# One 128-row weight transfer split into five transfers of 64, 24, 24, 8 and 8 rows, in a two-layer decode kernel on one core

## The chip, the core and the metric

The kernel runs on one core of one Trainium2 chip. The metric is device time in microseconds (us) of one launch; lower is better. The kernel before took 178.09 us, the median of three runs (177.34 to 178.23). The profile is of one more execution, whose own time was 177.7 us, with a span of 175.9 us from the first to the last instruction.

Five engines matter below: PE (matmul), DVE (vector), ACT (scalar), POOL, and SP, whose queue here does nothing but issue transfers from device memory (HBM) to on-chip memory (SBUF, 128 partitions). The transfers themselves are carried out by 16 DMA engines.

## What is computed

One token for each of four batch rows goes through attention and a gated feed-forward block, twice, with the same weights both times:

```python
def _A_ref(x, k_cache, v_cache, wq, wo):      # Hq 32, Hkv 8, Sk 8192, Dh 128; W = 2048
    q = (lambda x, *d: x.transpose(*d))((x @ wq).reshape(B, Sq, Hq, Dh), 0, 2, 1, 3)
    k = jnp.repeat(k_cache[:, :, Sk - W:, :], rep, axis=1)
    v = jnp.repeat(v_cache[:, :, Sk - W:, :], rep, axis=1)
    scores = jnp.einsum("bhqd,bhkd->bhqk", q, k) * (Dh ** -0.5)
    p = _softmax(scores, axis=-1)
    o = jnp.einsum("bhqk,bhkd->bhqd", p, v)
    return (lambda x, *d: x.transpose(*d))(o, 0, 2, 1, 3).reshape(B, Sq, Hq * Dh) @ wo
...
def _B_ref(x, w_gate, w_up, w_down):          # D 512, F 1792
    g = jnp.einsum("bsd,df->bsf", x, w_gate)
    u = jnp.einsum("bsd,df->bsf", x, w_up)
    h = _sigmoid(g) * u
    return jnp.einsum("bsf,fd->bsd", h, w_down)
...
x = x + _A_ref(_layernorm(x, axis=-1), A_k_cache, A_v_cache, A_wq, A_wo)
x = x + _B_ref(_layernorm(x, axis=-1), B_w_gate, B_w_up, B_w_down)
x = x + _A_ref(_layernorm(x, axis=-1), A_k_cache, A_v_cache, A_wq, A_wo)
x = x + _B_ref(_layernorm(x, axis=-1), B_w_gate, B_w_up, B_w_down)
```

Almost all the work is reading: 69.73 MB come from HBM in one launch. wq alone is 4 MB, each of the two cache windows 16 MB.

## The kernel before

The kernel is written as a list of operations with declared reads and writes (`P.op`, L52). A planner (`_schedule`, L92) puts them in an order for each engine, except for SP: there the transfers are issued in the order in which the code created them (L116 to L118). `_assign_sync` (L180) gives every SP transfer one of 24 semaphores in turn (L289) and lets a transfer wait until the one that used its semaphore before it, 24 transfers earlier, has landed (L197 to L202).

On-chip memory is an arena of 50 slots of 4 KB for each of 128 partitions. `tile_ap` (L384) is a pair of slots, 8 KB in each partition, 1 MB in all; `tok` (L387) names the two slots as what an operation writes or reads. Every transfer goes through `dma` (L396), which issues one `dma_start` at L399 on SP. So all SP transfers carry the line L399 in the profile.

A list `loads` holds the transfers that are still to be issued; `fill` (L450) issues from its head while there is a free tile. The list begins with the first read of wq (`load_wq(0)`, L1440), then comes K of the heads 0 to 2 (`load_k`, two 1 MB transfers each), then K, V and wo in turn (L1441 to L1450), the feed-forward weights, the second read of wq and so on. At the start the arena is empty, so that the first transfers are issued one behind the other with no wait.

The first read of wq is four blocks (`NC = 4`): block c holds rows 128c to 128c+127 of wq, one row of 4096 bfloat16 values (8 KB) in each partition. Each block is one transfer of 128 rows. `q_mms` (L793) multiplies: for block c, four matmuls of the normalised token (`xn`) with 512 columns each, at L804, accumulate over c. `q_first` (L826) runs this for the upper and lower half of the columns; the first four matmuls of a block wait for its transfer. Then come two transposes on DVE (L816), a multiply (L820), and on PE and ACT the spreading of q over the scores' layout (L851, L856). K tiles are transposed in place on DVE (L863), scores are built on PE (L881, L892), the softmax runs on DVE and ACT (L905 to L935), and P times V on PE at L982, which waits for V's transfers.

A tile that has been used up goes back to the pool and the next transfer of the list is issued into it, after a wait for the PE operation that read it last. From about 30 us on, most of SP's transfers wait in this way.

Of the kernel before, what the change touches and what calls it, by code (L numbers as in the profile page):

```python
# [254 lines left out]
class _SlotPool:  # L255
# [16 lines left out]
    bw_8k=421.0, bw_4k=409.0, bw_3k=405.0, bw_1k=347.0,  # L272
# [6 lines left out]
def build(nc, A_x, A_k, A_v, A_wq, A_wo, B_wg, B_wu, B_wd, out, cfg=None):  # L279
# [17 lines left out]
    NC = D // 128  # L297
# [15 lines left out]
    wq_d = A_wq.rearrange("(kt p) n -> p kt n", p=128)  # L313
# [9 lines left out]
    with es:  # L323
# [52 lines left out]
        def slot_ap(s):  # L376
            if s == SIDE:
                return side[:, 0:SLOT]
            return arena[:, s * SLOT:(s + 1) * SLOT]

        def stok(s, n=SLOT):
            return [("slot", s)] + (side_toks if s == SIDE else []) + ([("e", 0)] if s == SIDE and n > 1536 else [])

        def tile_ap(s):  # L384
            return arena[:, s * SLOT:(s + 2) * SLOT]

        def tok(s):  # L387
            return [("slot", s), ("slot", s + 1)]
# [7 lines left out]
        def dma(name, dst, src, w, r=(), rate="bw_4k", nbytes=None, sem=None):  # L396
            if nbytes is None:
                nbytes = dst.partition_size() * dst.free_nbytes()
            o = P.op("sync", name, 0.0, lambda e, dst=dst, src=src: e.dma_start(dst, src),  # L399
                     r=r, w=w, dma_bytes=nbytes, dma_rate=tm[rate])  # L400
            if sem is not None:
                o.sem = sem
                o.inc = 16
            return o


        loads = []
        where = {}
        left = {}
# [50 lines left out]
        def need(name):  # L460
            while name not in where:
                take_load()
            return where[name]

        def done(name):
            left[name] -= 1
            if left[name] == 0:
                s = where.pop(name)
                if name in on_free:
                    on_free[name](s)  # L470
                else:
                    pool.release(s)
                fill()
# [13 lines left out]
        def load_half(name, src, rate, size, where_):  # L487
            left[name] = 1
            homes[name] = [where_]
            on_free[name] = lambda s: hfree.add(s)  # L490

            def emit(s):
                dma(str(name), slot_ap(s)[:, 0:size], src, w=stok(s, size), rate=rate)
            loads.append((name, emit))

        def load(name, n_use, rate, part):
            left[name] = n_use

            def emit(s):
                src = part[1]  # L500
                dst = tile_ap(s)[:, 0:part[0]]
                if name[0] in ("wg", "wu"):
                    dst = tile_ap(s).rearrange("p (f n) -> p f n", f=2)[:, :, 0:F]
                elif len(src.shape) == 3 and not part[2]:
                    dst = dst.rearrange("p (f n) -> p f n", f=src.shape[1])
                dma(str(name), dst, src, w=tok(s), rate=rate)
            loads.append((name, emit))

        bounds = []
        f0 = 0  # L510
        while f0 < NFC:
# [9 lines left out]

        def load_wq(k):
            if k == 0:
                for c in range(NC):
                    load(("wq", c, k), 2, "bw_8k", (2 * SLOT, wq_d[:, c, :], False))
            else:
                for i in (1, 0):
                    for c in range(i, NC):
                        load_half(("wq", c, k, i), wq_d[:, c, i * SLOT:(i + 1) * SLOT], "bw_4k", SLOT,
                                  (((Y, 0), (Y, 1), (WQ, 1), (WQ, 0)), (None, (WQ, 0), (GA, 0), (SP, 0)))[i][c])  # L530

        def wq_part(k, c, i):

            if k == 0:
                return ("wq", c, k), i * SLOT
            return ("wq", c, k, i), 0
# [177 lines left out]
        o = P.op("scalar", "x_in", 1300.0, lambda e: e.dma_start(x_nat, x_d), w=[("prow",)])  # L714
# [78 lines left out]
        def q_mms(k, i, qb, cs):  # L793
            for c in cs:
                name, o = wq_part(k, c, i)
                s = need(name)

                src = slot_ap(s) if k else tile_ap(s)
                rd = stok(s) if k else tok(s)

                def e_q(pe, c=c, src=src, o=o):
                    last = None
                    for hh in range(4):
                        last = pe.matmul(ps[32 * hh:32 * hh + NB, qb, :], xn[:, c * NB:(c + 1) * NB],  # L804
                                         src[:, o + hh * 512:o + (hh + 1) * 512],
                                         start=(c == 0), stop=(c == NC - 1))
                    return last
                P.op("tensor", "q%d_%d_%d" % (k, i, c), 4 * tm["pe_row"], e_q,
                     r=rd + [("xn",)], w=[("qrow", i)], banks=(qb,))
                done(name)  # L810
# [15 lines left out]
        def q_first(variance):  # L826
            for n, i in enumerate((0, 1)):
                q_mms(0, i, OBS[n], range(NC))
                if n == 0:
                    variance()  # L830
                q_turn(0, i, OBS[n])

        def q_second(variance):
            q_mms(1, 1, WB, (0, 1))
            variance()
            unstash_half(tuple(named("ln_rd2Q")))
            q_mms(1, 1, WB, (2, 3))
            q_mms(1, 0, OBS[1], (0,))
            fresh.append(q_turn(1, 1, WB))
# [598 lines left out]
        stashed = ("V",) + keep[0] + (0,)  # L1438
        stay = keep[1:] + [(HKV - 2, 1)]
        load_wq(0)  # L1440
        for h in range(AHEAD):  # L1441
            loads.append((("K", h), lambda _, h=h: load_k(h)))
# [7 lines left out]
        load_wo(HKV // 2 - 1)  # L1450
        load_glu(0)
        load_wq(1)
        v_tiles = {}
        n_v = 0
# [16 lines left out]
        n = len(P.ops)  # L1471
# [44 lines left out]
def bass_interleave_layers__sliding_block_cached__glu_gated_glu__decode_kernel(  # L1516
    nc, A_x, A_k_cache, A_v_cache, A_wq, A_wo, B_x, B_w_gate, B_w_up, B_w_down, out,
):
    build(nc, A_x, A_k_cache, A_v_cache, A_wq, A_wo, B_w_gate, B_w_up, B_w_down, out)
# [28 lines left out]
```

## Time and profile before

| | us |
|---|---|
| median of three runs | 178.09 (177.34 to 178.23) |
| the profiled execution | 177.7 |
| its span | 175.9 |
| PE busy | 106.1 |
| DVE busy | 104.2 |
| ACT busy | 32.7 |
| POOL busy | 21.7 |
| bytes moved | 70.00 MB, mean 398 GB/s |

Busy time is time in which an engine executed instructions; waiting is not counted, nor is issuing a transfer. In the profile "L863 DVE" is an instruction of line 863 on DVE, and "arena<-in_A_wq_dram" is a transfer from wq into the arena. Beside this page the trace keeps one record for each packet that a DMA engine moved, with its queue, size, start and length, and the time of every semaphore update; a row of 8 KB is one packet, and each engine ends its part of a transfer with a packet of 4 bytes, the end mark that updates the semaphore. The lines on which the forecast rests are shown in it.

### The profile page before, as it was taken

What the parts mean: (1) busy time and instruction counts of PE and PEld (TensorE: products, weight loads), DVE (VectorE), ACT (ScalarE), POOL (GpSimd) and SP (SyncE); (2) the same over time, 40 slices, a digit from 0 to 9 for tenths busy, and PEclk for the clock granted to TensorE, in tenths of its full rate; (3) what the DMA queues carried; (4) which work ended last, traced back from release to release, by engine and by line L of the source; (5) the groups of instructions that cost most, each with busy time, mean ns of one, the idle gap of its engine ahead of it and who ended that gap; (6) DMA issues with size and microseconds to landing.
All of it is one profiled execution on the core that took longest, in us unless ns stands there. A gap on an engine that the chain in (4) does not pass through costs nothing.

```text
span 175.9 us, 3909 instructions
## 1 busy us (share of the span) xinstructions
PE 106.1 (60%) x1653; PEld 54.2 (31%) x1653; DVE 104.2 (59%) x256; ACT 32.7 (19%) x87; POOL 21.7 (12%) x89
## 2 busy tenths in 40 slices
PE   0536256269566282661765466547987999776663
PEld 0203112014334051340444452142322444425321
DVE  6307997994957748377322381316299999733351
ACT  2002022322303003020030000100133455430011
POOL 6100010101101001010010000000011553342000
PEclk9999999999999999999999999999999999965576
DMA  5999999999999999999999999999999999999990
GB/s 180 419 436 423 419 421 427 404 428 423 415 415 412 417 428 421 427 404 427 417 414 425 408 399 403 412 407 388 402 366 408 425 419 419 421 417 401 411 376 31
DMA packets 12738, 70.00 MB, mean 398 GB/s; under 512 B 1320, under 2 KB 1328, under 8 KB 6576
## 3 DMA queue, kind: packets, MB, share of 16 engines
q1 hardware_dynamic: 12712, 69.74, 97.4%
q8 instruction: 13, 0.21, 0.5%
q14 instruction: 5, 0.04, 0.1%
q10 hardware_dynamic: 8, 0.00, 0.0%
HBM read 69.73 MB, written 0.00 MB: 396 GB/s over the span
## 4 chain that ended last, share of the span: by engine, by line
DMA 47%; DVE 33%; PE 15%; issue 2%; SPq 1%; POOL 1%; ACT 0%; DVEq 0%
DMA arena<-in_A_v_cache_dram 19%; DMA arena<-in_B_w_down_dram 13%; DVE arena L863 12%; DMA arena<-in_A_wq_dram 10%; PE ps L892 7%; DMA arena<-in_B_w_gate_dram 5%; DVE small L905 5%; PE ps L881 2%; DVE arena L1073 2%; DVE small L909 2%; DVE side L913 2%; DVE side L940 2%; DVE arena L1078 1%; DVE arena L593 1%; DVE small L917 1%
## 5 line engine op out<-in xcount | busy, mean ns | idle before, releaser
L863 DVE STREAM_TRANSPOSE arena<-arena 128x1024 f32<-128x1024 f32 x32 | 37.0, 1205 | 0.1
L982 PE MATMUL ps<-side,arena 128*128 128x8 bf16 x576 | 18.2, 168 | 13.4 <-DMA arena<-in_A_v_cache_dram 13.4
L892 PE MATMUL ps<-arena,side 128*32 128x512 bf16 x256 | 25.2, 527 | 0.0
L982 PEld LDWEIGHTS ps<-side,arena 128*128 128x128 bf16 x576 | 16.8, 104 | 19.7 <-DMA arena<-in_A_v_cache_dram 17.2
L905 DVE TENSOR_REDUCE small<-ps 128x1 f32<-128x512 f32 x16 | 10.8, 676 | 17.6 <-PE ps L892 17.5
L920 ACT ACTIVATE side<-ps,small 128x512 bf16<-128x512 f32 x16 | 11.0, 687 | 36.7 <-PE ps L1000 18.4
L881 PE MATMUL ps<-small,msk_s 128*32 128x512 bf16 x64 | 8.6, 526 | 14.3 <-DVE arena L863 13.7
L856 ACT CAST side<-ps 128x256 bf16<-128x256 f32 x16 | 5.9, 370 | 34.7 <-PE ps L892 25.8
L892 PEld LDWEIGHTS ps<-arena,side 128*32 128x32 bf16 x256 | 8.3, 120 | 10.2 <-issue 7.5
L935 ACT CAST side<-ps 128x512 bf16<-128x512 f32 x16 | 9.4, 585 | 10.8 <-PE ps L933 10.8
L933 PE MATMUL ps<-side,perm 128*128 128x512 bf16 x16 | 8.1, 507 | 5.0 <-ACT side L920 4.9
L949 POOL CAST small<-small 128x1 bf16<-128x1 f32 x9 | 1.7, 187 | 76.2 <-ACT side L920 76.2
L804 PE MATMUL ps<-arena,xn 128*4 128x512 bf16 x60 | 7.7, 574 | 3.9 <-DMA arena<-in_A_wq_dram 3.6
L782 ACT ACTIVATE small<-ps 128x4 f32<-128x4 f32 x4 | 0.7, 173 | 47.8 <-PE ps L778 47.8
L1354 PE MATMUL ps<-arena,xn 128*4 128x448 bf16 x60 | 7.1, 530 | 3.1 <-DMA arena<-in_B_w_up_dram 1.5
L1064 PE MATMUL ps<-arena,side 128*32 128x512 bf16 x112 | 8.2, 416 | 0.2 <-DVE small L917 0.2
L940 DVE STREAM_TRANSPOSE side<-side 128x256 f32<-128x256 f32 x16 | 6.9, 433 | 2.2 <-ACT side L935 2.0
L851 PE MATMUL ps<-side,eyew 32*128 32x64 bf16 x64 | 5.6, 217 | 3.4 <-ACT side L856 2.4
L881 PEld LDWEIGHTS ps<-small,msk_s 128*32 128x32 bf16 x64 | 1.7, 98 | 17.2 <-DVE arena L863 15.8
L816 DVE STREAM_TRANSPOSE side<-ps 128x512 f32<-128x512 f32 x3 | 2.2, 717 | 8.2 <-PE ps L804 8.1
L990 DVE TENSOR_TENSOR onb<-ps,rinv 128x16 bf16<-128x16 f32 x9 | 1.7, 185 | 8.9 <-PE ps L982 8.6
L1363 DVE STREAM_TRANSPOSE side<-ps 128x448 f32<-128x448 f32 x4 | 2.5, 636 | 6.7 <-PE ps L1354 6.7
(119 smaller groups left out, 135.5 us busy)
## 6 DMA issues: line engine op xcount, KB each, us to landing
arena<-in_A_v_cache_dram SPq DMA_DIRECT2D x27, 1024.0 KB, 18.9
arena<-in_A_k_cache_dram SPq DMA_DIRECT2D x16, 1024.0 KB, 24.9
arena<-in_A_wq_dram SPq DMA_DIRECT2D x4, 1024.0 KB, 8.1
arena<-in_A_wo_dram SPq DMA_DIRECT2D x3, 1024.0 KB, 26.5
arena<-in_A_wq_dram SPq DMA_DIRECT2D x6, 512.0 KB, 6.3
arena<-in_B_w_up_dram SPq DMA_DIRECT2D x4, 448.0 KB, 6.2
arena<-in_B_w_gate_dram SPq DMA_DIRECT2D x2, 896.0 KB, 21.9
arena<-in_B_w_up_dram SPq DMA_DIRECT2D x2, 896.0 KB, 22.8
```

Of the source, the lines that this page charges most:

```text
L804: last = pe.matmul(ps[32 * hh:32 * hh + NB, qb, :], xn[:, c * NB:(c + 1) * NB], src[:, o + hh * 512:o + (hh + 1) * 512], start=(c == 0), s ...
L863: P.op("vector", "T%d_%d" % (h, t), c_dve(1024), lambda v, v32=v32: v.transpose(v32, v32), r=[("slot", 4 * h + t)], w=[("slot", 4 * h + t)])
L881: last = pe.matmul(ps[32 * gi:32 * gi + 32, bank, :], msk_s[:, :], msk_m[:, :].unsqueeze(1).broadcast_to([128, 256, 2]), start=True, stop= ...
L892: last = pe.matmul(ps[32 * gi:32 * gi + 32, bank, :], qbd[:, q0:q0 + 32], kt[:, cp // 2, cp % 2, jh * NJ:(jh + 1) * NJ, :], start=False, s ...
L905: lambda v: v.tensor_reduce(nmax[:, k2:k2 + 1], ps[:, bank, :], AXX, ALU.max),
L920: lambda a: a.activation(prow[:, :].rearrange("p (m x t) -> p m x t", x=32, t=2), ps[:, bank, :].rearrange("p (m t x) -> p m x t", x=32, t ...
L933: lambda pe: pe.matmul(ps[:, pb, :], perm[:, :], prow[:, :], start=True, stop=True),
L935: P.op("scalar", "pc" + tag, c_act(512), lambda a: a.copy(prow[:, :], ps[:, pb, :]), r=[("ppb", pb)], w=[("prow",)], banks=(pb,))
L940: P.op("vector", "pt" + tag, c_dve(256), lambda v: v.transpose(et, prow[:, :].bitcast(F32)), r=[("prow",)], w=[("e", k2)])
L982: last = pe.matmul(ps[:, ob, bp * 8:bp * 8 + 8], src[:, j * 128:(j + 1) * 128], ev[:, j % 2, j % 16 // 2, x0:x0 + 8], start=(j == 0), stop ...
L1064: last = pe.matmul(ps[32 * g:32 * g + 32, ob, :], ew[:, g, mq, t], src.rearrange("p (m t d) -> p t m d", t=2, d=128)[:, t], start=(n == 0) ...
L1354: last = pe.matmul(ps[32 * g:32 * g + NB, gub[n], 0:NF], xn[:, c * NB:(c + 1) * NB], slot_ap(s)[:, g * NF:(g + 1) * NF], start=(c == 0), s ...
```

## The change

The fourth block of the first read of wq (c = 3) no longer comes as one transfer of 128 rows. It comes as five, of the rows 0 to 63, 64 to 87, 88 to 111, 112 to 119 and 120 to 127, issued one behind the other in the place of the one, into the same tile and the same partitions as before. The first of them takes the place of the old one among the tokens (it "writes" both slots of the tile); the other four get tokens of their own, and the same dependencies as the first. The operation of PE that multiplies this block reads all five tokens, so it waits for five semaphores instead of one.

```diff
+        ROWS = (0, 64, 88, 112, 120, 128)
+
+        def load_rows(name, n_use, src):
+            left[name] = n_use
+
+            def emit(s):
+                first = None
+                for n, (a, b) in enumerate(zip(ROWS[:-1], ROWS[1:])):
+                    o = dma("%s_%d" % (name, a), tile_ap(s)[a:b, :], src[a:b, :], w=[("rows", n)] if n else tok(s), rate="bw_8k")
+                    if n:
+                        o.deps.update(first.deps)
+                    else:
+                        first = o
+            loads.append((name, emit))
...
             if k == 0:
-                for c in range(NC):
+                for c in range(NC - 1):
                     load(("wq", c, k), 2, "bw_8k", (2 * SLOT, wq_d[:, c, :], False))
+                load_rows(("wq", NC - 1, k), 2, wq_d[:, NC - 1, :])
             else:
...
                 rd = stok(s) if k else tok(s)
+                if not k and c == NC - 1:
+                    rd = rd + [("rows", n) for n in range(1, len(ROWS) - 1)]
```

On PE, DVE, ACT and POOL the same instructions stand in the same order in both kernels. On SP there are four transfers more, ahead of the first transfer of K; all that follow keep their order. As semaphores are dealt out in turn, every later transfer uses the one four places further on.

## The prediction

> **What bounds the kernel now.** I read the page from the top: busy shares, slices, transfer queues; then the table by stretches, the chain of waits in order of time, the first 20 us of the timeline, and the packet records.
>
> ```profile
> PE 106.1 (60%) x1653; PEld 54.2 (31%) x1653; DVE 104.2 (59%) x256; ACT 32.7 (19%) x87; POOL 21.7 (12%) x89
> DMA  5999999999999999999999999999999999999990
> GB/s 180 419 436 423 419 421 427 404 428 423 415 415 412 417 428 421 427 404 427 417 414 425 408 399 403 412 407 388 402 366 408 425 419 419 421 417 401 411 376 31
> q1 hardware_dynamic: 12712, 69.74, 97.4%
> q8 instruction: 13, 0.21, 0.5%
> q10 hardware_dynamic: 8, 0.00, 0.0%
> ```
>
> No engine is busy for more than 60% of the span; the 16 DMA engines are busy in every slice but the first and last, and SP's own queue (q1) alone fills 97.4% of them. The table by stretches (its columns: length, busy time of each engine, clock, DMA share, GB/s) shows where they are short of work:
>
> ```profile
> 13.30:63.00 49.70, 27.56 (x349) 12.23 (x350) 38.85 (x65) 9.80 (x24) 3.77 (x20) 1.00 1.01 420
> 90.00:120.00 30.00, 16.53 (x339) 11.22 (x340) 10.12 (x31) 1.31 (x5) 0.36 (x2) 1.00 1.02 409
> 120.00:135.00 15.00, 12.38 (x130) 4.12 (x130) 10.33 (x28) 3.91 (x11) 1.15 (x5) 1.00 1.01 387
> ```
>
> Only from 120 to 135 us does the rate fall clearly, to 387 GB/s against 420: (1 - 387/420) x 15 = 1.2 us of lost reading. Everywhere else a microsecond of DMA time lost is a microsecond of the kernel. The chain says how far ahead the queue runs (start, length, what):
>
> ```profile
> 2.19 11.09 DMA arena<-in_A_wq_dram
> 13.33 0.60 PE ps L804 x4
> 16.30 4.54 DVE arena L863 x4
> 63.98 22.92 DMA arena<-in_A_v_cache_dram
> 87.99 11.30 DMA arena<-in_A_v_cache_dram
> 116.47 6.65 DMA arena<-in_A_wq_dram
> 155.70 16.72 DMA arena<-in_B_w_down_dram
> ```
>
> The chain runs over DVE and PE from 13 to 64 us, but the transfer issued at 63.98 lands 22.92 us later: about nine transfers stand ahead of it, so a delay of DVE of a few us would cost nothing there. The depth shrinks to 6.65 us at 116 and is 16.72 us again at the end. What the end waits for, all the way, is the reading. The changed transfer is the fourth that SP issues. The timeline shows the issues and PE's waits for the blocks of wq (in brackets the idle time before, and what ended it):
>
> ```profile
> 0.79 2.03 SPq L399 DMA_DIRECT2D arena<-in_A_wq_dram  x4
> 2.86 6.21 SPq L399 DMA_DIRECT2D arena<-in_A_k_cache_dram  x8
> 8.36 0.10 PEld L804 LDWEIGHTS ps<-arena,xn 128*4 128x4 bf16 x8 [1.01 <-DMA arena<-in_A_wq_dram]
> 10.84 0.10 PEld L804 LDWEIGHTS ps<-arena,xn 128*4 128x4 bf16 x8 [2.37 <-DMA arena<-in_A_wq_dram]
> 13.33 0.09 PEld L804 LDWEIGHTS ps<-arena,xn 128*4 128x4 bf16 x4 [2.39 <-DMA arena<-in_A_wq_dram]
> ```
>
> Blocks land 2.48 us apart (10.84 - 8.36; 13.33 - 10.84 = 2.49): 128 rows on 16 engines are 8 rows each, 2.48 / 8 = 0.31 us a row, which is also the length of a row's packet (0.309). An engine has one row under way and begins the next 3 ns before the last ends. So the rows can be followed engine by engine, and **each engine is its own queue**: what delays one is made up nowhere unless it runs out of work. The 13 instruction reads of q8 show it: each holds one engine for about 1.05 us, the next row then takes 0.8 instead of 0.31, and that engine stays some 1.6 us behind. The 16 engines end the fourth block of wq within 0.4 us, but the last transfer between 170.98 and 173.06 us: eight within 0.6 us of the first, eight 1.4 to 2.1 us behind it. The semaphore waits for the last.
>
> **The change part by part.** The sum is made against the profiled 177.7 us (span 175.9 and 1.8 around it), which is 0.4 us under the median of 178.09.
>
> *Bytes:* the same 128 rows of 8 KB. *SP:* four issues more of 0.41 to 0.63 us (shortest and longest issue of wq), so K's first issue moves from 2.86 to 4.5 to 5.4 us; all transfers behind it move too, until the queue is full (the issue at 7.52 us already takes 1.5 us for that). The engines reach K at about 12.4 us: hidden by three blocks of wq. Without that cover it would be 1.6 to 2.5 us. *Semaphores:* each transfer now waits for one 24 places back in a list longer by four; the first such wait, at about 31 us, is for a block of wq landed at 6 us: nothing. *End marks:* four more of 9 ns on an engine: 0.04 us. *PE:* five semaphores instead of one ahead of the matmuls of c = 3; with 0.04 to 0.05 us an issue step (the chain's "issue" pieces), 0.2 us. Behind it stand L778 and the second half of L804, for which DVE's L816 waits: on the DVE chain, not on the reading.
>
> *Which engine moves what.* A 128-row transfer leaves 16 end marks with 8 rows to each. The x load (4 rows) leaves 8 packets in q10, four rows and four marks: one row on each of four engines. So a transfer is cut into equal shares. If 64, 24 and 8 rows are cut likewise (16 shares of 4, 12 of 2, 8 of 1) and always begin with the same engine, eight engines get 4+2+2+1+1 = 10 rows, four get 8 and four get 4: +0.62, 0 and -1.24 us. The trace shows no transfer of 24 or 8 rows. [...]
>
> *What a narrow transfer costs.* The disputed term. All large transfers here span 128 partitions. **Lower bound:** rows keep 0.31 us wherever they go, and only the shares above count: between -0.6 and +0.6 at the end (rivals). **Upper bound:** what limits a row is the way into its group of partitions, ways in proportion to rows; then every transfer, however narrow, takes the 2.48 us of a full one: 5 x 2.48 - 2.48 = +9.9. The nearest row is the x load: its four rows of 1 KB took 0.044 us, two at a time, about half of a 2-KB row (0.084), which speaks for the lower end; but 4 KB in all may rest in buffers that 512 KB does not fit. Between ends this far apart I take the middle, **+5.0 us**.
>
> [...]
>
> *Where it goes.* Eight engines have to take all five in turn and are then 5 us behind; each K, V and weight transfer lands when its last engine does. They never run dry before 120 us, so nothing is made up. The DVE chain starts with q and K, both later by the same 5 us. The 1.2 us lost from 120 to 135 belong to engines that had run ahead; the late ones do not gain there. Sum: 177.7 + 5.0 + 0.0 = 182.7, against the median 178.09 + 5.0 = **183.1; I say 183.0**, with 181.0 to 184.8 for this case.
>
> **The rivals.**
>
> *Rows only move between engines (no price for narrowness).* The end moves by the shares: if one of the late engines is among the eight, +0.62, if none, down. For it: the x packets. The two x engines that can be told by their starts (first wq row at 1.86 and 1.88 us, 6 ns behind an end mark of x) were, as far as packets can be followed, delayed by instruction reads, one at 88.2, the other at 125.4 and 144.2; and x's four engines belong to the eight if the cut begins with the same engine. So +0.2: 178.3 (177.7 to 178.9).
>
> *A smaller price.* Narrowness counts for the 64 rows alone (2.48 instead of 1.24: +1.24), the short ones overlap with K, plus the 0.62 of shares: 180.0 (179.0 to 181.0).
>
> *Faster.* Place: the end of each transfer. The late eight are the four engines relieved by 1.24 us and the four that are unchanged, the early eight those that get 0.62. Then the latest end moves from 2.1 to 1.5 us behind the first: -0.6; with a smaller spread part of the 1.2 us lost from 120 to 135 returns, -0.4 by a third of it: 177.1 (176.3 at most). It decides from the point where no late engine is among the eight. Against it: the two x engines above, and that instruction reads hit eight different engines one after the other before 120 us.
>
> **How the numbers follow.** A measurement of this kernel can tell about 0.5% (0.9 us) from no change. Chances: forecast 0.55, smaller price 0.12, rows only 0.22, faster 0.11. Slower by over 0.5% is the first two, 0.67; within 0.5% 0.22; faster 0.11. The range leaves out the faster case and some 0.07 above (the upper bound is 188, for which I see little): 177.6 to 184.8.
>
> **What would show it.** Right: the wait at L804 for the last block ends near 18 instead of 13.3 us; the GB/s of the first three slices falls; the landings of K all stand some 5 us later; eight engines' end marks lie 5 us behind the others for the rest of the run. Wrong: the wait ends at 13 to 14 us and row packets keep 0.31 us: then narrowness has no price, and the end marks' spread at 20 us (1.9 us in that case, 0.62 + 1.24) tells which engines are which.

## The result and the profile after

| | before | after |
|---|---|---|
| median of four runs each, us | 178.16 (177.34 to 178.49) | 184.03 (183.78 to 184.58) |
| ratio, 95% interval | | 1.0341 (1.0298 to 1.0383) |
| the profiled execution, us | 177.7 | 183.9 |
| its span, us | 175.9 | 182.2 |

The kernel is 5.9 us slower; the interval makes that 5.3 to 6.8 us. In the code after the change, L804 is now L822, L816 is L834, L863 is L881, L892 is L910 and L982 is L1000. From the page of the profile after, busy times, slices and SP's queue:

```profile
PE 106.7 (59%) x1653; PEld 54.6 (30%) x1653; DVE 104.2 (57%) x256; ACT 32.7 (18%) x87; POOL 21.7 (12%) x89
DMA  5999999999999999999999999999999999999990
GB/s 192 426 266 138 397 421 421 423 412 419 423 424 413 419 416 419 424 415 415 421 417 423 419 396 402 398 394 405 380 312 410 419 426 419 417 416 408 407 366 26
q1 hardware_dynamic: 12752, 69.74, 97.0%
```

The engines' work is what it was. SP's queue moved the same bytes, but its packets took 97.0% of 182.2 us = 176.7 us of 16 engines' time, against 97.4% of 175.9 = 171.3 before: 5.4 us more. The rate falls in the third and fourth slice (9.1 to 18.2 us), to 266 and 138 GB/s; the row "DMA" above it shows 9 all the same. Only one later slice stands out, the 30th (132 to 137 us), with 312 where before has 366. The table by stretches says it for the stretch in which the five transfers move. First the kernel before, then the one after (length, PE, PEld, DVE, ACT, POOL, clock, DMA share, GB/s):

```profile
11.00:19.20 8.20, 3.65 (x30) 1.38 (x22) 4.85 (x7) 1.12 (x4) 0.00 (x0) 1.00 1.01 426
```

```profile
11.00:19.20 8.20, 1.02 (x9) 0.14 (x9) 0.00 (x0) 0.00 (x0) 0.00 (x0) 1.00 1.00 181
19.20:30.00 10.80, 5.49 (x46) 2.20 (x46) 9.57 (x12) 1.49 (x5) 0.00 (x0) 1.00 1.01 421
120.00:135.00 15.00, 11.52 (x132) 4.96 (x132) 6.27 (x19) 1.90 (x6) 0.00 (x0) 1.00 1.03 382
```

A DMA share of 1.00 at 181 GB/s: the DMA engines always have a packet under way, but the packets take longer. Lost in these 8.2 us: (1 - 181/426) x 8.2 = 4.7 us. After it the rate is back, and from 120 to 135 us it is no better than the 387 of before: nothing is made up. The work of that stretch comes some 5.4 us later now, and from 125.4 to 140.4 us the rate is 368. The timeline of the kernel after shows SP's issues and PE's waits for the blocks of wq:

```profile
0.79 4.34 SPq L399 DMA_DIRECT2D arena<-in_A_wq_dram  x8
5.17 5.19 SPq L399 DMA_DIRECT2D arena<-in_A_k_cache_dram  x8
8.19 0.10 PEld L822 LDWEIGHTS ps<-arena,xn 128*4 128x4 bf16 x8 [0.84 <-DMA arena<-in_A_wq_dram]
11.11 0.10 PEld L822 LDWEIGHTS ps<-arena,xn 128*4 128x4 bf16 x8 [2.82 <-DMA arena<-in_A_wq_dram]
19.20 0.59 PE L822 MATMUL ps<-arena,xn 128*4 128x512 bf16 x4 [7.06 <-DMA arena<-in_A_wq_dram]
```

The third block is multiplied at 11.11 (before 10.84), the fourth at 19.20 (before 13.33): it comes 5.9 us later. The chain of waits carries that to the end, with the same links as before:

```profile
4.81 14.26 DMA arena<-in_A_wq_dram
22.17 4.54 DVE arena L881 x4
69.83 22.63 DMA arena<-in_A_v_cache_dram
93.55 11.31 DMA arena<-in_A_v_cache_dram
121.90 6.86 DMA arena<-in_A_wq_dram
163.23 15.53 DMA arena<-in_B_w_down_dram
```

Against before the links stand 5.9 us later at the first L881, the same at 69.83, 5.6 at 93.55, 5.4 at 121.90, and the last one lands at 178.76 against 172.42: 6.3. From the records of packets and semaphore updates, the length of a row's packet (8 KB; median) by when it began, and when the last engine's end mark came:

```
row packets that began in     10.5-12.5   12.5-15   15-17.5   from 20 us on
before                          309 ns     309 ns    309 ns        312 ns
after                           618 ns     819 ns   1104 ns        312 ns     (longest 1199 ns)

landing, us       block c=2   64 rows   24 rows   24 rows   8 rows   8 rows   first K
before              10.79     13.28 (128 rows)                                15.77
after               11.07     13.62     15.29     16.96     18.27    19.06    21.23
```

The 64 rows alone take as long as the whole block took. The other four add 1.68, 1.66, 1.32 and 0.79 us, which is 5.45 us; the first K transfer is 5.46 us late.

### The profile page after: what moved, and what is told of

It is laid out like the page before. It is cut to its first block, busy times and chain, and to the rows that moved or that the text cites. A ratio compares the mean times of both kernels' runs of the same rounds, so it can differ in the third digit from the quotient of the medians.

```text
span 182.2 us, 3918 instructions
## 1 busy us (share of the span) xinstructions
PE 106.7 (59%) x1653; PEld 54.6 (30%) x1653; DVE 104.2 (57%) x256; ACT 32.7 (18%) x87; POOL 21.7 (12%) x89
## 4 chain that ended last, share of the span: by engine, by line
DMA 47%; DVE 31%; PE 15%; issue 2%; SPq 2%; POOL 1%; ACT 0%; DVEq 0%
DMA arena<-in_A_v_cache_dram 19%; DMA arena<-in_B_w_down_dram 12%; DVE arena L881 12%; DMA arena<-in_A_wq_dram 12%; PE ps L910 7%; DVE small L923 5%; DMA arena<-in_B_w_gate_dram 5%; PE ps L899 2%; SPq L399 2%; DVE arena L1091 2%; DVE small L927 2%; DVE side L931 2%; DVE side L958 2%; DVE arena L1096 1%; DVE arena L609 1%
## 5 line engine op out<-in xcount | busy, mean ns | idle before, releaser
L881 DVE STREAM_TRANSPOSE arena<-arena 128x1024 f32<-128x1024 f32 x32 | 36.9, 1203 | 0.1
L1000 PE MATMUL ps<-side,arena 128*128 128x8 bf16 x576 | 18.2, 168 | 13.5 <-DMA arena<-in_A_v_cache_dram 13.5
L910 PE MATMUL ps<-arena,side 128*32 128x512 bf16 x256 | 25.8, 538 | 0.0
L1000 PEld LDWEIGHTS ps<-side,arena 128*128 128x128 bf16 x576 | 16.7, 104 | 19.9 <-DMA arena<-in_A_v_cache_dram 17.4
L822 PE MATMUL ps<-arena,xn 128*4 128x512 bf16 x60 | 7.6, 573 | 10.1 <-DMA arena<-in_A_wq_dram 9.8
L910 PEld LDWEIGHTS ps<-arena,side 128*32 128x32 bf16 x256 | 8.3, 121 | 10.3 <-issue 7.8
L953 ACT CAST side<-ps 128x512 bf16<-128x512 f32 x16 | 9.4, 585 | 10.5 <-PE ps L951 10.5
L834 DVE STREAM_TRANSPOSE side<-ps 128x512 f32<-128x512 f32 x3 | 2.1, 717 | 14.1 <-PE ps L822 14.0
```

The lines of the kernel that those rows point to most:

```text
L881: P.op("vector", "T%d_%d" % (h, t), c_dve(1024), lambda v, v32=v32: v.transpose(v32, v32), r=[("slot", 4 * h + t)], w=[("slot", 4 * h + t)])
L910: last = pe.matmul(ps[32 * gi:32 * gi + 32, bank, :], qbd[:, q0:q0 + 32], kt[:, cp // 2, cp % 2, jh * NJ:(jh + 1) * NJ, :], start=False, s ...
L953: P.op("scalar", "pc" + tag, c_act(512), lambda a: a.copy(prow[:, :], ps[:, pb, :]), r=[("ppb", pb)], w=[("prow",)], banks=(pb,))
L1000: last = pe.matmul(ps[:, ob, bp * 8:bp * 8 + 8], src[:, j * 128:(j + 1) * 128], ev[:, j % 2, j % 16 // 2, x0:x0 + 8], start=(j == 0), stop ...
```

## The experiments

All are the changed kernel with another cut of the fourth block of wq. `PARTS` below lists (rows, columns) of the transfers in the order of issue, with a:b written for a slice; SP issues them and PE waits for them as in the changed kernel, and all the rest is the same. The edit common to them, and then one list each:

```diff
-        ROWS = (0, 64, 88, 112, 120, 128)
+        PARTS = [...]
...
-                for n, (a, b) in enumerate(zip(ROWS[:-1], ROWS[1:])):
-                    o = dma("%s_%d" % (name, a), tile_ap(s)[a:b, :], src[a:b, :], w=[("rows", n)] if n else tok(s), rate="bw_8k")
+                for n, p in enumerate(PARTS):
+                    o = dma("%s_%d" % (name, n), tile_ap(s)[p], src[p], w=[("rows", n)] if n else tok(s), rate="bw_8k")
...
-                    rd = rd + [("rows", n) for n in range(1, len(ROWS) - 1)]
+                    rd = rd + [("rows", n) for n in range(1, len(PARTS))]
```

Three theories stood after the result. *Ways*, of the kind of the prediction's upper bound: rows that go at the same time to the same part of the 128 partitions share one way in, and each is slower by the number that share it (two on one way: twice 309 ns); how the partitions would be divided among ways no run shows. *Number*: each transfer costs something as such (about 1.5 us, 5.9 over four). *Shares*: what counts is that some engines get more rows than others. cols5, two64, eight16 and eight16s ran beside a kernel before with a median of 177.71 us, the other four beside one with 177.77.

**cols5: five transfers, each over all 128 partitions**

```diff
+PARTS = [(:, 0:2048), (:, 2048:2816), (:, 2816:3584), (:, 3584:3840), (:, 3840:4096)]
```

> The fourth block comes as five transfers again, but cut by columns: each spans all 128 partitions, with 4096, 1536, 1536, 512 and 512 bytes of every row. [...] Number: every transfer more costs the same, whatever its shape, (184.03 - 178.16) / 4 = 1.5 us: +5.9, 184.0. Shares: the cost came from engines with unequal numbers of rows; here all engines move the same: +0, 178.2.

178.66 us, ratio 1.0051 (1.0031 to 1.0070): +0.95 us. As many issues and semaphores as in the changed kernel, more end marks (80 against 56), and less than a sixth of its loss. In the table of slices of cols5 the dip is nearly gone:

```profile
GB/s 183 426 318 432 424 421 419 409 425 423 421 415 412 420 426 423 417 411 420 424 419 421 408 400 405 403 406 373 393 410 419 417 424 423 415 415 405 407 376 27
```

Number falls. By estimate from the packets of before (4 KB 0.159 us, 2 KB 0.084) the smaller pieces come to 8 x (0.159 + 2 x 0.065 + 2 x 0.03) = 2.8 us instead of 2.48, +0.3; the 0.95 is more than that. The packets say where it is: the pieces of 1.5 KB took 65 ns and those of 0.5 KB 27, but the 4-KB pieces of the first of the five took 245 ns in the mean, where other 4-KB packets take 159 at the median and 165 in the mean: 8 x 0.08 = 0.6 us or a little more for each engine. Why they do was not tried.

**two64 and four32: two or four transfers of neighbouring rows**

```diff
+PARTS = [(0:64, :), (64:128, :)]                                      # two64
+PARTS = [(0:32, :), (32:64, :), (64:96, :), (96:128, :)]          # four32
```

> The fourth block comes as two transfers, rows 0 to 63 and 64 to 127; every engine moves 4 rows of each. Ways: each of the two reaches half of the ways, so 8 rows pass each way in turn, 2.48 us a transfer: 4.96 instead of 2.48, +2.5 us, 180.6 (180.0 to 181.4). Number: one transfer more, +1.5, 179.6. Shares: equal, +0, 178.2.

> Four transfers of 32 neighbouring rows, two rows to each engine. [...] If the price follows the narrowness of a transfer (64 rows +2.2 in all, 16 rows +5.2): between them, about +3.7.

two64: 179.91 us, ratio 1.0122 (1.0094 to 1.0150), +2.20. four32: 180.18 us, ratio 1.0124 (1.0094 to 1.0154), +2.41. Row packets took 0.62 us in two64 (median 609 to 621 ns) and 0.60 in four32 (604 to 606), twice the 309 of a full transfer. So transfers half as wide, and twice as many, cost 0.2 us more, which the intervals (0.5 us to either side) do not tell from nothing. Of two64 that is what Ways expected, 2.48 us for four rows of each engine, 0.62 a row. In four32 the rows are no slower for being of narrower transfers, so that the price does not follow the narrowness alone (about +3.7 was expected of that); and the upper bound's 2.48 us for every transfer, 3 x 2.48 = +7.4 here, is far off.

**eight16 and eight16s: the same eight transfers of 16 rows, neighbouring and eight apart**

```diff
+PARTS = [(16*i:16*i+16, :) for i in range(8)]                            # eight16
+PARTS = [(i:128:8, :) for i in range(8)]                                 # eight16s
```

> The fourth block comes as eight transfers of 16 neighbouring rows (0 to 15, 16 to 31 and so on); every engine moves one row of each. [...] Number: seven transfers more, 7 x 1.5 = +10.3, 188.4. Shares: equal, +0, 178.2.

> As the eight transfers of 16 neighbouring rows, but each takes every eighth row (0, 8, 16 ... 120; then 1, 9, 17 ... and so on). The number of transfers, their rows, the packets and each engine's one row of each are the same; only the partitions differ. [...] Number, and any theory in which the place in on-chip memory does not count: the same time as with neighbouring rows.

eight16: 183.02 us, ratio 1.0291 (1.0258 to 1.0324), +5.31. eight16s: 180.14 us, ratio 1.0133 (1.0105 to 1.0162), +2.43. Number of transfers, rows in each, shares of the engines (one row of each transfer), issues and semaphores are the same; only which rows go together differs, and with it the partitions. From the slices of eight16, then of eight16s:

```profile
GB/s 200 428 215 157 415 421 425 419 409 420 428 417 417 415 418 423 414 423 414 425 415 421 417 400 404 399 401 404 347 393 416 421 430 419 414 419 401 409 370 31
```

```profile
GB/s 192 429 277 328 424 416 424 414 416 424 424 415 417 423 413 424 416 416 419 426 415 429 405 400 406 402 410 398 398 390 400 426 426 416 416 415 404 413 350 20
```

The fourth slice has 157 GB/s against 328. PE's wait for the block, in the two timelines:

```profile
18.57 0.60 PE L822 MATMUL ps<-arena,xn 128*4 128x512 bf16 x4 [5.93 <-DMA arena<-in_A_wq_dram]
```

```profile
15.95 0.60 PE L822 MATMUL ps<-arena,xn 128*4 128x512 bf16 x4 [3.86 <-DMA arena<-in_A_wq_dram]
```

The wait ends 2.62 us apart, the kernels 2.88. Rows took 875 ns in eight16 and 596 to 610 in eight16s. This is the clearest of the runs: place alone makes 2.9 us, and neither Number nor Shares has anything to say to it. One thing it leaves open: a row's place in HBM goes with its partition in all these runs, and no run moved the one without the other. So it is not shown that the on-chip side sets the price; the 0.62 us a row of two64, expected from Ways, agrees with it. The rows of eight16 took 2.8 times 309 ns, and no run shows why that number and not another. The trace of eight16 shows the landings of neighbouring transfers 0.6 to 0.9 us apart while each is spread over 1.6 to 1.9 us: at least two of them are in flight at once, on different partitions.

**spread5: the changed kernel's five sizes, rows two apart**

```diff
+PARTS = [(0:128:2, :), (1:48:2, :), (49:96:2, :), (97:112:2, :), (113:128:2, :)]
```

> Same five transfers in number and size (64, 24, 24, 8, 8 rows), hence the same shares of the engines, but of rows two apart: 0,2..126; 1,3..47; 49..95; 97..111; 113..127. [...] Number or shares alone: nothing changes, +5.9 as in the changed kernel.

180.75 us, ratio 1.0167 (1.0130 to 1.0205): +2.98, where 5.9 was expected of Number and of Shares. With the same 64, 24, 24, 8 and 8 rows and the same shares, half the loss goes with the place. The 64 rows, every second one, kept 309 ns (618 for the 64 neighbouring ones of the changed kernel) and landed 1.6 us behind the third block; the four small transfers then took 3.75 us more. Why the 64 rows were not slowed here, and the rows eight apart of eight16s were, is open. The stretch of the dip in spread5, and PE's wait:

```profile
11.00:19.20 8.20, 2.94 (x26) 1.18 (x18) 2.07 (x5) 0.75 (x3) 0.00 (x0) 1.00 1.01 321
```

```profile
16.11 0.59 PE L822 MATMUL ps<-arena,xn 128*4 128x512 bf16 x4 [4.44 <-DMA arena<-in_A_wq_dram]
```

**eq5: five transfers with equal shares**

```diff
+PARTS = [(0:64, :), (64:80, :), (80:96, :), (96:112, :), (112:128, :)]
```

> Five transfers of neighbouring rows, 64 and four of 16, so that each of the 16 engines has an equal share (4+1+1+1+1 = 8 rows). [...] If five transfers cost as such, whatever the shares: +5.9.

181.40 us, ratio 1.0199 (1.0160 to 1.0237): +3.63. That is near the sum of measured prices: 64 rows by two64 (2.48 + 2.20) / 2 = 2.34 us, 16 rows by eight16 (2.48 + 5.31) / 8 = 0.97, 2.34 + 4 x 0.97 - 2.48 = +3.7. So of the 5.87 of the changed kernel, 2.2 come with cutting the upper 64 rows as 24, 24, 8, 8 instead of four times 16. How this splits is seen in the table below: the changed kernel has 1.5 us more than eq5 in the column "rows" and 2.1 in "first K", so most of it is slower rows.

**rev5: the changed kernel's five in reverse order**

```diff
+PARTS = [(120:128, :), (112:120, :), (88:112, :), (64:88, :), (0:64, :)]
```

> The changed kernel's five transfers in reverse order (rows 120 to 127 first, 0 to 63 last). [...] If the price came from what stands behind the narrow ones (the transfers of K that meet the last of them), the 64 rows at the end would cover it: about +3.

182.00 us, ratio 1.0260 (1.0201 to 1.0318): +4.23; the interval (3.6 to 5.7 us) does not take in the 3 expected if the price came from the transfers of K behind. By the medians the order counts for some 1.6 us, but the interval touches that of the changed kernel (5.3 to 6.8).

The packets of rev5 show that sharing a way is not the whole of it. Of the rows that began from 10.5 to 12.5 us, on all engines, none took less than 700 ns, and the longest took 1339, 4.3 times 309. Yet four engines then had only rows of the 64-row transfer, which they end at 13.9 to 14.1 us, 2.2 us ahead of the next engine, while the narrow rows beside them were all of 64 to 127; with no narrower transfer beside them, in two64, rows of a 64-row transfer took 609 to 621. So narrow transfers slow rows that go elsewhere too. By what, no run shows.

**All of them side by side.** "Rows" is the time that the 8-KB packets before 22 us took above 309 ns each, less the same of before (13.0 us), over 16 engines; "first K" is when the last engine's end mark of the first K transfer came, later than before (15.77 us):

```
us           rows   first K   time of the kernel
two64        2.37     2.32      2.20
four32       2.51     2.31      2.41
eight16s     2.22     2.44      2.43
spread5      1.52     2.42      2.98
eq5          3.21     3.39      3.63
rev5         3.52     4.27      4.23
eight16      4.68     5.22      5.31
after        4.75     5.46      5.87
cols5         -       0.96      0.95
```

Two things are read from it. The last two columns agree within 0.25 us in seven of nine rows, and within 0.6 in all: what the queue of reads lost by 22 us is what the kernel loses, whatever the cut. And in the rows with equal shares "first K" stays within 0.25 us of "rows", but for eight16 (0.54), while it is 0.7 to 0.9 more in spread5, rev5 and after. "Rows" is a mean over the engines, and K lands with the latest one: these 0.7 to 0.9 us are roughly what unequal shares add (eight16, with equal shares, has 0.54 as well).

## Why the prediction was right

**The bound.** Right: the reading is what the end waits for, and its loss passes on in full (the two columns above), from 21 us to the end. Of the signs named, PE's wait for the last block ended at 19.20 us (near 18 was forecast), and K landed 5.5 us later; the GB/s fell in the third and fourth slice, not in the first two.

**Bytes, SP, semaphores, end marks, PE.** Right, as far as the runs resolve them. K's first issue stands at 5.17 us, inside 4.5 to 5.4, and the first engines come to K more than 7 us later. two64, four32 and eight16s, with 2, 4 and 8 transfers and rows of about the same length (596 to 621 ns), lie within 0.23 us, so that a transfer more, with its issue, semaphore, wait and end marks, costs about 0.04 us; by the far ends of the intervals of two64 and eight16s it is 0.2 us at most.

**Which engine moves what.** Right. The semaphores of the five count 16 updates from engines for the 64 rows, and 13, 13, 9 and 9 updates in all for the others, one of which comes at the issue (at 4.18, 4.60, 4.94 and 5.31 us): 12, 12, 8 and 8 engines.

**The price of narrowness.** The upper bound was right in the main in that the place of the rows counts: rows took 875 ns in eight16 and 596 to 610 in eight16s. That sharing a way is the cause is not shown, and rev5 shows that it does not explain all of it. Its size was a choice, the middle between 0 and +9.9, and that the forecast came within 1.1 us is luck: nothing in the prediction said that the truth lies near that middle. The lower bound rested on the x load, four rows of 1 KB that were not slowed; its 0.044 us a row said nothing of 8-KB rows, and the buffers spoken of beside it no run shows. The upper bound took every transfer for as long as a full one. Measured are 2.55 us for the 64 rows and 1.68, 1.66, 1.32 and 0.79 for the rest. The longest row took 1199 ns, 3.9 times 309; the longest of rev5 took 1339.

Nor does narrowness as such set the price: 32 neighbouring rows (four32, 604 to 606 ns) are no slower than 64 (two64, 609 to 621 ns), 16 rows eight apart take 596 to 610 ns and 16 neighbouring ones 875. With unequal shares the changed kernel lost 5.87, with equal shares, and four times 16 rows, eq5 lost 3.63.

**The step that failed** is "Eight engines have to take all five in turn and are then 5 us behind", and with it "eight engines' end marks lie 5 us behind the others for the rest of the run". At the first K transfer the end marks spread over 2.1 us, not 5: the earliest engine was itself 3.8 us later than before, the latest 5.5. Eight end last, within 0.2 us of each other, but the other eight were slowed too. In the packets from 15 to 17.5 us, when at least four engines had no row of the last four transfers left and could only be on K, the shortest 8-KB row took 851 ns. So the narrow transfers slow K's rows with their own; a transfer takes its price from its neighbours in the queue as well. I had reckoned each engine as a queue for itself and left out that the rows of different engines slow each other. It changed the forecast of the end by little, since the end goes by the latest engine.

**From 5.5 to 6.3.** Between the first K and the last transfer of the profiled execution the delay grew, though not steadily. With the first instruction read (36 us) the landings came 5.74 us later than before, and the spread of the end marks went from 2.1 to 3.6 us; from 115 to 127 us the delay was back at 5.4, and the spread went down to 1.7. The growth comes behind that: from 5.6 us at the landing of 133.8 us to 6.4 at the next, 135.9 us, in the slice with 312 GB/s, where the DMA share is below 1 (0.96 from 131 to 137 us, against 1.03 from 120 to 135), so that engines stood without work for a part of it. This was seen in one trace of each kernel and not tested.

**The rivals.** "Rows only move between engines" and "faster" fall with the row packets of 1.1 us. "A smaller price", with the short transfers overlapping K at no cost, falls with the landings: the four short ones took 5.45 us. Its 2.48 us for the 64 rows was right.

## What to carry to other kernels

In a kernel that waits for its reads, look at which rows go together in a transfer, not only at how many bytes or transfers there are: eight transfers of 16 rows cost 2.4 us with rows eight apart (eight16s) and 5.3 with neighbouring ones (eight16). A transfer that must be cut is cut by columns, over all 128 partitions (+0.95 us for five pieces, against +5.9 by rows). A DMA share near 1 (1.01 at 426 GB/s, 1.00 at 181) does not show that the reading is at its best; the GB/s of the stretch and the length of one row's packet (309 ns, and 618 to 1104 in the dip) do.

## What was not expected of the hardware

- The profile's DMA share stays at 1.00 while the rate falls from 426 to 181 GB/s: an engine whose row is held up counts as busy.
- Narrow transfers slow the full ones that follow them in the queue: no 8-KB row that began from 15 to 17.5 us took less than 851 ns, and four engines at least were on K by then.
- They slow rows for other partitions as well: in rev5 no row from 10.5 to 12.5 us took less than 700 ns, and four engines then had only rows of 0 to 63 while the narrow ones went to 64 to 127.
- 16 neighbouring rows, one for each engine, took 875 ns each in eight16, where the upper bound gives every transfer 2.48 us, and at least two such transfers were in flight at once.
- 4-KB pieces of full-width transfers took 245 ns in the mean where they cut an 8-KB row and 165 elsewhere; the cause is open.
